# Loading half of x transposed by DMA, fewer remainders of P by DMA, and an output added in place, in a two-problem cached attention kernel

## The chip, the cores and the metric

The kernel runs on one core of one Trainium2 chip. Its time is the time of one execution on the device in microseconds (us). Three runs of the kernel before took 718.01, 720.44 and 720.60 us, with a median of 720.44. Profiles come from one execution each, which the hardware profiler recorded. Engine names in a profile: PE is the matrix engine TensorE (PEld its weight load), DVE is VectorE, ACT is ScalarE, POOL is GpSimd, SP is SyncE, and a "q" behind a name is the engine's queue, which waits and issues DMAs.

## The reference

Two independent problems A and B of the same shape are computed and their outputs stand side by side. B=16 batches, 80 query rows each, D=576, 32 query heads on 16 key/value heads of 512 cached positions, head size 128, all in bf16:

```python
def _A_ref(x, k_cache, v_cache, wq, wo):
    B, Sq, D = x.shape                      # 16, 80, 576
    Hq, Dh = 32, 128
    rep = Hq // k_cache.shape[1]            # 2
    q = (x @ wq).reshape(B, Sq, Hq, Dh).transpose(0, 2, 1, 3)
    k = jnp.repeat(k_cache, rep, axis=1)
    v = jnp.repeat(v_cache, rep, axis=1)
    scores = jnp.einsum("bhqd,bhkd->bhqk", q, k) * (Dh ** -0.5)
    p = _softmax(scores, axis=-1)
    o = jnp.einsum("bhqk,bhkd->bhqd", p, v)
    return o.transpose(0, 2, 1, 3).reshape(B, Sq, Hq * Dh) @ wo
# out = concatenate([A_ref(...), B_ref(...)], axis=-1)   # (16, 80, 1152)
```

## The kernel before

**Steps.** The work is cut into 128 steps, 64 for each problem. One step is one batch with four key/value heads, so 8 query heads of 80 rows, 640 rows in all. A key/value head has 160 query rows: 128 of them are a tile of their own, and the 32 left over of each of the four heads are packed into a fifth tile, the remainder. For each of the five tiles TensorE computes scores of 128 x 512 (L678, the remainder L665), VectorE takes the negative maximum (L687), ScalarE the exponential with the row sum (L691), VectorE the reciprocal (L697), and GpSimd multiplies P by it (L700).

**P turned around.** P times V needs P transposed. For every step TensorE issues small transposes of 64 x 64 blocks against an identity matrix (L733), 8 for each of the five tiles, 40 in a full step; they land in PSUM, and VectorE or ScalarE copies them to `pT` (the four main tiles in two copies, L751 and L752, the remainder in two, L757 and L758). In steps from `RT0` to `RT1` that are odd (`RTM`), the remainder goes another way: SyncE issues a transposing DMA from `p_sb` to `pT` (L740), the step on TensorE has 32 small transposes, and the remainder's two copies are left out. `RT0` is 71, so 27 steps go that way. The remainder's tile of P has four slots (`NPR`), which are used again four steps later. Then come P times V (L781) and the copy of the result to `oT` (L795).

**Projections.** q is projected for four batches and one pair of heads at a time: four matmuls per head over the first 512 of the 576 columns of x (L542, "Q"), and a tail for the last 64 columns (L555, "QT"), in which the two heads use the two halves of the array. Early on, the tails are operations of their own; later they are part of a step's small transposes. The scaled copy to `qT` (L568, L569) is on ScalarE or VectorE. The weights of the first two groups of heads come in four pieces each (L507) with the two tail pieces `wt` (L511).

**x.** The projection needs x transposed, `xT`, in two halves of eight batches (640 rows, five blocks of 128). For problem A a half is loaded plainly into the memory of `acc` (L380) in two parts, three blocks and two; GpSimd doubles the last 64 columns (L388), TensorE transposes the blocks (L401) and the last columns (L419), and VectorE copies them to `xT` (L406, L423). For problem B the first 512 columns come by one transposing DMA for each half (L436), and the last 64 columns by two plain DMAs into `xst` (L441, L442), five transposes (L456) and three copies (L461 to L463).

**Output.** `oT` times wo is summed over two groups of heads (L827). The first group's result is copied to `acc` (L839), the second group's is added to it by VectorE and written as bf16 to a buffer `osb` of two slots (L856), from which SyncE stores it (L862).

**Order.** There is no planner at run time. Every operation is added to a list with a stream's name, and a long string `ORDER` says, letter by letter, which stream's next operation comes next (a digit is the PSUM bank it gets, a quote sends it to the second of two engines). Each engine runs its own operations in that order. Semaphore waits are worked out from what operations read and write. So each engine, TensorE and SyncE's queue too, works strictly in order, and an operation that waits holds all behind it on that engine. At the start SyncE issues the first part of x, the first piece of wq, the second part of x, the rest of the first two groups' wq, and then the first K (L631, a transposing DMA of 1,024 rows by 512).

## Time and profile before

| | us |
|---|---|
| median of three runs | 720.44 |
| the profiled execution | 720.92 |
| its span, first to last instruction | 719.0 |
| TensorE busy | 712.0 (99%) |
| VectorE busy | 630.0 (88%) |
| ScalarE busy | 637.5 (89%) |
| GpSimd busy | 431.9 (60%) |

The page of the profile gives for each engine the busy time and for each group of instructions the count, the mean duration in ns and the idle time just before them with what ended it. "Busy" of TensorE is modelled, since matmuls overlap. Times in rows count from the start of the span. The small transposes of step 64, the first of problem B, start at 375 us, those of step 71 at 416 (its transposing DMA at 413.43), those of step 97 at 555.

### The profile page before, as it was taken

What the parts mean: (1) busy time and instruction counts of PE and PEld (TensorE: products, weight loads), DVE (VectorE), ACT (ScalarE), POOL (GpSimd) and SP (SyncE); (2) the same over time, 40 slices, a digit from 0 to 9 for tenths busy, and PEclk for the clock granted to TensorE, in tenths of its full rate; (3) what the DMA queues carried; (4) which work ended last, traced back from release to release, by engine and by line L of the source; (5) the groups of instructions that cost most, each with busy time, mean ns of one, the idle gap of its engine ahead of it and who ended that gap; (6) DMA issues with size and microseconds to landing.
All of it is one profiled execution on the core that took longest, in us unless ns stands there. A gap on an engine that the chain in (4) does not pass through costs nothing.

```text
span 719.0 us, 25863 instructions
## 1 busy us (share of the span) xinstructions
PE 712.0 (99%) x10604; PEld 508.8 (71%) x10604; DVE 630.0 (88%) x1419; ACT 637.5 (89%) x1830; POOL 431.9 (60%) x650
## 2 busy tenths in 40 slices
PE   9999999999999999999999999999999999999998
PEld 5576777777777777777777776767677777777777
DVE  3999998899978998899998899878898889998995
ACT  1999998899988998799988999888999898998994
POOL 0467657566655765755774566645676466665783
PEclk9999999999999999999999999999999999999999
DMA  9999999999799998999999999999999999999970
GB/s 238 275 217 240 273 252 250 286 232 244 175 268 241 220 241 194 258 223 240 255 216 248 226 201 206 228 246 239 220 229 204 279 196 261 225 247 221 211 195 18
DMA packets 388853, 164.23 MB, mean 228 GB/s; under 512 B 293248, under 2 KB 385664, under 8 KB 388736
## 3 DMA queue, kind: packets, MB, share of 16 engines
q1 hardware_dynamic: 388736, 162.59, 100.2%
q8 instruction: 84, 1.38, 0.8%
q14 instruction: 33, 0.27, 0.2%
HBM read 87.65 MB, written 2.95 MB: 126 GB/s over the span
## 4 chain that ended last, share of the span: by engine, by line
PE 93%; DMA 2%; DVE 2%; ACT 1%; SPq 0%; issue 0%; ACTq 0%; DVEq 0%
PE ps L827 22%; PE ps L781 20%; PE ps L542 18%; PE ps L678 15%; PE ps L733 10%; PE ps L665 5%; PE ps L555 4%; DVE negmax L687 2%; DMA pT<-p_sb 1%; DMA wq_sb<-in_A_wq_dram 1%; DMA out_dram<-osb 1%; ACT p_sb L691 0%; ACT qT L568 0%; DVE xT L406 0%; DVE qT L569 0%
## 5 line engine op out<-in xcount | busy, mean ns | idle before, releaser
L700 POOL TENSOR_SCALAR p_sb<-p_sb,rinv 128x512 bf16<-128x512 bf16 x640 | 430.1, 692 | 271.4 <-DVE rinv L697 270.8
L691 ACT ACTIVATE p_sb<-ps,negmax 128x512 bf16<-128x512 f32 x640 | 442.7, 713 | 27.3 <-DVE negmax L687 23.5
L687 DVE TENSOR_REDUCE negmax<-ps 128x1 f32<-128x512 f32 x640 | 419.2, 682 | 35.0 <-PE ps L678 30.3
L781 PE MATMUL ps<-pT,v_sb 128*128 128x160 bf16 x2048 | 191.2, 233 | 1.1 <-ACT p_sb L691 0.8
L781 PEld LDWEIGHTS ps<-pT,v_sb 128*128 128x128 bf16 x2048 | 152.8, 98 | 42.6 <-ACT p_sb L691 4.1
L827 PE MATMUL ps<-wo_sb,oT 128*128 128x288 bf16 x1280 | 181.1, 286 | 0.0
L678 PE MATMUL ps<-kT,qT 128*128 128x512 bf16 x512 | 178.0, 380 | 1.2 <-ACT p_sb L691 0.8
L542 PE MATMUL ps<-xT,wq_sb 128*128 128x320 bf16 x1024 | 174.4, 299 | 0.2 <-DMA wq_sb<-in_A_wq_dram 0.2
L827 PEld LDWEIGHTS ps<-wo_sb,oT 128*128 128x128 bf16 x1280 | 122.0, 98 | 42.5 <-ACT p_sb L691 0.8
L691 ACT ACTIVATION_READ_ACCUMULATOR p_sb<-ps,negmax 128x1 f32 x640 | 146.0, 228 | 0.0
L542 PEld LDWEIGHTS ps<-xT,wq_sb 128*128 128x128 bf16 x1024 | 95.4, 98 | 45.0 <-ACT p_sb L691 2.4
L751 ACT COPY pT<-ps 128x512 f32<-128x512 f32 x157 | 92.4, 602 | 13.3 <-PE ps L733 12.8
L733 PEld LDWEIGHTS ps<-ident,p_sb 64*128 64x128 bf16 x4904 | 88.2, 95 | 7.3 <-issue 1.3
L733 PE MATMUL ps<-ident,p_sb 64*128 64x64 bf16 x4904 | 92.4, 190 | 0.3 <-issue 0.2
L752 DVE COPY pT<-ps 128x1024 bf16<-128x1024 bf16 x99 | 67.3, 684 | 11.4 <-PE ps L733 10.0
L568 ACT ACTIVATE qT<-ps 128x320 bf16<-128x320 f32 x133 | 59.0, 458 | 19.3 <-PE ps L555 15.5
L569 DVE TENSOR_SCALAR qT<-ps 128x320 bf16<-128x320 f32 x123 | 58.2, 482 | 10.7 <-PE ps L555 6.1
L795 DVE CAST oT<-ps 128x320 bf16<-128x320 f32 x122 | 58.4, 482 | 7.7 <-PE ps L781 7.4
L678 PEld LDWEIGHTS ps<-kT,qT 128*128 128x128 bf16 x512 | 48.0, 97 | 24.1 <-ACT p_sb L691 4.1
L795 ACT CAST oT<-ps 128x320 bf16<-128x320 f32 x134 | 58.9, 451 | 5.2 <-PE ps L781 4.9
L697 DVE RECIPROCAL rinv<-rowsum 128x3 f32<-128x3 f32 (+1 forms) x256 | 38.4, 160 | 1.8 <-ACT p_sb L691 1.7
L665 PE MATMUL ps<-kT,qT 128*32 128x512 bf16 x512 | 39.2, 384 | 0.0
(31 smaller groups left out, 175.5 us busy)
## 6 DMA issues: line engine op xcount, KB each, us to landing
v_sb<-in_A_v_cache_dram SPq DMA_DIRECT2D x64, 512.0 KB, 5.0
v_sb<-in_B_v_cache_dram SPq DMA_DIRECT2D x64, 512.0 KB, 5.2
wo_sb<-in_A_wo_dram SPq DMA_DIRECT2D x8, 576.0 KB, 5.8
wo_sb<-in_B_wo_dram SPq DMA_DIRECT2D x8, 576.0 KB, 5.8
wq_sb<-in_B_wq_dram SPq DMA_DIRECT2D x4, 1024.0 KB, 6.9
out_dram<-osb SPq DMA_DIRECT2D x40, 72.0 KB, 3.8
wq_sb<-in_A_wq_dram SPq DMA_DIRECT2D x8, 256.0 KB, 4.7
wq_sb<-in_A_wq_dram SPq DMA_DIRECT2D x2, 1024.0 KB, 8.4
```

Source lines behind the costliest of these rows:

```text
L542: last = e.matmul(ps[:, vbq[h].phys, QO:QO + 320], lhsT=wq_sb[:, wsl, ck, hi * 128:(hi + 1) * 128], rhs=xT[:, half, ck, n0:n0 + 320], star ...
L665: last = e.matmul(ps[32 * g4:32 * g4 + 32, vb_.phys, :], lhsT=qT[:, qsl_, bl_, g4 * 160 + 128:g4 * 160 + 160], rhs=k_of(U_, g4), start=Tru ...
L678: return e.matmul(ps[:, vb.phys, :], lhsT=qT[:, qsl, bl, gl * 160:gl * 160 + 128], rhs=k_of(U, gl), start=True, stop=True)
L687: return e.tensor_reduce(negmax[:, si:si + 1], ps[:, vb.phys, :], axis=AX.X, op=AluOpType.max, negate=True)
L691: return e.activation(p_sb[:, psl, :], ps[:, vb.phys, :], AF.Exp, bias=negmax[:, si:si + 1], scale=1.0, accum_out=rowsum[:, ss, k:k + 1])
L700: return e.tensor_scalar(p_sb[:, psl, :], p_sb[:, psl, :], rinv[:, ss, k:k + 1], 1.0, op0=AluOpType.mult, op1=AluOpType.mult)
L733: last = e.matmul(dst, lhsT=p_sb[64 * h:64 * h + 64, psls[k_], j * 128:(j + 1) * 128], rhs=ident[64 * h:64 * h + 64, 64 * h:64 * h + 64], ...
L751: return e.copy(dst.bitcast(F32), ps[:, vtp[h].phys, :].rearrange("p (j n) -> p j n", j=4))
L752: return e.tensor_copy(dst, psb[:, vtp[h].phys, :].rearrange("p (j n) -> p j n", j=4))
L781: last = e.matmul(ps[:, vo.phys, off:off + 160], lhsT=v_sb[:, vs, gl, j * 128:(j + 1) * 128], rhs=pT[:, pts, j, :, 32 * gl:32 * gl + 32], ...
L795: return (e.copy if en == "act" else e.tensor_copy)(dst, src)
L827: last = e.matmul(ps[:, vb.phys, 0:DC], lhsT=oT[:, sp_ * (HH // 2) + i, rb * 128:(rb + 1) * 128], rhs=wo_sb[:, 2 * c3 + sp_, i, :], start= ...
```

## The change

Three things change in the code, and the order string is written anew from its first to its last letter.

1. The first half of A's x (eight batches) is no longer loaded plainly and turned on TensorE. The first 512 columns come by two transposing DMAs, for the first three blocks and for the last two, and these are issued on ScalarE's queue. The last 64 columns come as in problem B. The first K, also a transposing DMA but on SyncE's queue, now waits until both have landed. The second half of A's x is loaded as before.
2. `RT0` goes from 71 to 97: the remainders of the odd steps from 71 to 95 go through TensorE; 14 steps are left that use the DMA.
3. The last addition writes its bf16 result into the first half of the memory of the sums that it reads, and the stores read from there; `osb` is gone, and with it the wait for one of its slots.

```diff
-RT0 = 71
+RT0 = 97
+XENG0 = ("act", "act")
...
-        for half in range(NPP):
+        for half in range(1, NPP):
             x_ap = probs[0][0]
...
-        for half in range(NPP):
-            x_ap = probs[1][0]
-
-            def em_ldxt(e, x_ap=x_ap, half=half):
-                src = x_ap.rearrange("b s d -> (b s) d")[half * NROW:(half + 1) * NROW, :]
-                return e.dma_start_transpose(xT[:, half, 0:4, :], src[:, 0:512].rearrange("n (c d) -> n c d", c=4))
+        for xi, (xp, half) in enumerate(((0, 0), (1, 0), (1, 1))):
+            x_ap = probs[xp][0]
+            nm = str(half) if xp else "00"
+            k_ = XA if xi == 0 else 5.0 * (UPR + 16 * half - LQ) - XK[half]
+
+            def em_ldxt(e, k0, k1, x_ap=x_ap, half=half):
+                src = x_ap.rearrange("b s d -> (b s) d")[half * NROW + k0 * 128:half * NROW + k1 * 128, :]
+                return e.dma_start_transpose(xT[:, half, 0:4, k0 * 128:k1 * 128],
+                                             src[:, 0:512].rearrange("n (c d) -> n c d", c=4))
...
+            for part, (k0, k1) in enumerate(((0, 3), (3, 5)) if xi == 0 else ((0, 5),)):
+                S.add(XENG0[part] if xi == 0 else "sp", (-100.0, -85.0)[part] if xi == 0 else k_,
+                      lambda e, k0=k0, k1=k1, f=em_ldxt: f(e, k0, k1),
+                      writes=[R(("xT", half, b_), xp) for b_ in range(k0, k1)], dsem="d_x%d%d" % (half, part),
+                      name="ldxt%s" % nm + (".%d" % part if xi == 0 else ""), stream="xa" if xi == 0 else "x")
...
                 S.add("sp", 5.0 * gfirst[U] + 0.5 * (U - gfirst[U]) - LA - KK, em_ldk,
+                      reads=[R(("xT", 0, b_), 0) for b_ in range(NRT)] if U == 0 else [],
                       writes=[R(("kT", (U + i_) % NK), U + i_) for i_ in range(kw)],
...
-                                return e.tensor_tensor(osb[:, slot, :], ps[:, vb.phys, 0:DC],
+                                return e.tensor_tensor(xs[:, rb, 2 * c3 * DC:(2 * c3 + 1) * DC], ps[:, vb.phys, 0:DC],
                                                        acc[:, rb, c3 * DC:(c3 + 1) * DC], AluOpType.add)
...
-                                return e.dma_start(dst, osb[:, slot, :])
+                                return e.dma_start(dst, xs[:, rb, 2 * c3 * DC:(2 * c3 + 1) * DC])
```

In the new order string TensorE's first operations are: the warm-up, the projection of the first pair of heads, the five transposes of the last columns, the first tail, then the projection of the second pair. Before, they were the warm-up, x's transposes, the projections of three pairs of heads, and then the first three tails. SyncE's first operations are now the first piece of wq, its two tail pieces, the two small loads of x's last columns, the remaining wq, and the first K.

## The prediction

> **What bounds the kernel now.** I read the busy shares of the engines first, then the chain that ended last, then a table of stretches, and only then single rows.

> ```profile
> PE 712.0 (99%) x10604; PEld 508.8 (71%) x10604; DVE 630.0 (88%) x1419; ACT 637.5 (89%) x1830; POOL 431.9 (60%) x650
> PE 93%; DMA 2%; DVE 2%; ACT 1%; SPq 0%; issue 0%; ACTq 0%; DVEq 0%
> core 0: us, PE busy (x) PEld busy (x) DVE busy (x) ACT busy (x) POOL busy (x), PEclk, DMA share, GB/s
> 0.00:7.00 7.00, 5.68 (x32) 3.20 (x33) 1.67 (x6) 1.28 (x1) 1.32 (x8) 1.00 0.75 204
> 7.00:20.00 13.00, 12.48 (x96) 7.42 (x93) 5.15 (x14) 2.52 (x7) 0.00 (x0) 1.00 1.18 264
> 20.00:36.00 16.00, 15.59 (x168) 8.84 (x166) 16.00 (x37) 15.89 (x47) 8.38 (x13) 1.00 1.17 273
> 36.00:413.00 377.00, 376.88 (x5819) 270.98 (x5816) 341.99 (x779) 349.48 (x1012) 233.40 (x349) 1.00 1.03 238
> 413.00:556.00 143.00, 141.33 (x2106) 100.42 (x2104) 125.16 (x277) 130.06 (x374) 91.21 (x136) 1.00 1.04 221
> 556.00:717.00 161.00, 160.05 (x2400) 117.96 (x2397) 140.02 (x311) 138.29 (x392) 97.60 (x146) 1.00 0.94 209
> ```

> TensorE is the bound. Its granted clock is 1.00 throughout, and from 36 to 413 us it is idle 377.00 - 376.88 = 0.12 us. Over 0 to 717 it idles about 5 us in all (the six rows add up to 712.01 busy). So the change can move the end in three places only: the work on TensorE itself, the first 36 us, and the stretch 413 to 556, where it idles 143.00 - 141.33 = 1.67 us. That stretch holds steps 71 to 97, whose odd steps send their remainders by DMA today.

> **The remainders, steps 71 to 97.** Thirteen odd steps (71, 73 ... 95) go back to TensorE: 8 more small transposes each, and two evictions in place of one DMA.

> ```profile
> 690.16 0.69 PE ps L733 x40
> 694.00 0.57 PE ps L733 x32
> L757 ACT COPY pT<-ps 128x128 f32<-128x128 f32 x106 | 28.5, 284 | 7.6 <-PE ps L733 7.0
> L758 DVE COPY pT<-ps 128x256 bf16<-128x256 bf16 x96 | 26.1, 283 | 7.3 <-PE ps L733 6.5
> ```

> In the chain a step with 40 transposes takes 0.69 us and one with 32 takes 0.57. TensorE gets 13 x 0.12 = 1.56 us more, all on the path. The 26 evictions are 26 x 0.284 = 7.4 us over VectorE and ScalarE. In 413 to 556 these two have 286 - 125.16 - 130.06 = 30.8 us free, which is the cover, and I cost them at nothing: from 36 to 413 every remainder goes through TensorE and it still never waits. If the cover were gone, half of them on either engine would be 3.7 us.

> What leaves with the 13 DMAs is their waits: two pieces of the chain, an issue, and the three TensorE rows after them.

> ```profile
> 413.43 4.13 DMA pT<-p_sb
> 510.62 5.67 DMA pT<-p_sb
> 478.87 1.23 SPq L740 DMA_TRANSPOSE pT<-p_sb  x1
> 418.48 0.39 PE L678 MATMUL ps<-kT,qT 128*128 128x512 bf16 x1 [0.17 <-ACT p_sb L691]
> 483.85 0.44 PE L781 MATMUL ps<-pT,v_sb 128*128 128x160 bf16 x4 [0.81 <-ACT p_sb L691]
> 517.21 0.39 PE L678 MATMUL ps<-kT,qT 128*128 128x512 bf16 x1 [0.46 <-ACT p_sb L691]
> ```

> The first and third follow a transfer that held a slot of P which the next exponential wanted. Before the second stands the DMA issued at 478.87: 483.85 is 5 us later, like the 4.13 and 5.67 above, and the row names ScalarE, which had long been done. I take out 0.17 + 0.81 + 0.46 = 1.44 us; the rest of the 1.67 has other causes. What is late next is TensorE's own work. So this part is +1.56 - 1.44 = +0.12 us, and SyncE's queue loses 13 issues that nobody waits for.

> **The start.** SyncE loses two x loads and gains two small loads of the last 64 columns; ScalarE, idle then, gains the two transposing loads. TensorE loses 25 transposes and gains 5; GpSimd loses two copies; VectorE loses 7 copies and gains 3. Nothing was behind GpSimd's. In SyncE's queue, the next fence, 0.45 and 0.50 go and about as much comes in, so what stands behind keeps its time but for the wait below.

> ```profile
> 0.79 0.45 SPq L380 DMA_DIRECT2D acc<-in_A_x_dram  x1
> 1.30 0.48 SPq L507 DMA_DIRECT2D wq_sb<-in_A_wq_dram  x1
> 1.82 0.50 SPq L380 DMA_DIRECT2D acc<-in_A_x_dram  x1
> 2.37 1.38 SPq L511 DMA_DIRECT2D wt<-in_A_wq_dram  x2
> ...
> 10.01 5.71 SPq L631 DMA_TRANSPOSE kT<-in_A_k_cache_dram  x1
> 3.79 4.45 DMA wq_sb<-in_A_wq_dram
> 8.37 2.33 PE L542 MATMUL ps<-xT,wq_sb 128*128 128x320 bf16 x16 [0.16 <-DMA wq_sb<-in_A_wq_dram]
> 19.45 0.38 PE L678 MATMUL ps<-kT,qT 128*128 128x512 bf16 x1 [0.36 <-ACT qT L568]
> 19.76 0.31 PE L555 MATMUL ps<-xT,wt 64*128 64x320 bf16 x2
> ```

> Now the second piece of the projection goes on at 8.37, when its weights have landed (3.79 + 4.45), and the first scores start at 19.45. In the new order the first projection tail comes before the second piece's matmuls. TensorE works in order, so everything behind that tail waits for the small loads, five transposes and three copies. Their prices are those of the same operations for problem B:

> ```profile
> xst<-in_B_x_dram SPq DMA_DIRECT2D x1, 80.0 KB, 4.1
> xT<-in_B_x_dram SPq DMA_TRANSPOSE x1, 7.1
> xst<-in_B_x_dram SPq DMA_DIRECT2D x1, 16.0 KB, 7.6
> 237.83 0.44 PE L456 MATMUL ps<-ident,xst 128*128 128x128 bf16 x5
> 238.95 0.47 DVE L461 COPY xT<-ps 64x640 bf16<-64x640 bf16 x1
> ...
> 239.79 0.22 DVE L463 COPY xT<-ps 64x128 bf16<-64x128 bf16 x1
> kT<-in_A_k_cache_dram SPq DMA_TRANSPOSE x1, 9.3
> DMA to landing us min/median/max: 6.1/8.4/13.4
> acc<-in_A_x_dram SPq DMA_DIRECT2D x2, 288.0 KB, 4.6
> ```

> The small loads are issued after wq's first piece and two of wt: 0.79 + 0.48 + 1.38 and gaps, about 2.8, the second at 3.4 (I give each of them 0.6, near wt's 1.38 / 2). Landing takes between 4.1 and 7.6 us by the two xst rows. I take 4.1, since the 7.6 stood behind megabytes of another load and here only 384 KB are ahead: 7.5. Then 0.44 for the transposes, 239.79 + 0.22 - 238.95 = 1.06 for the copies, 0.3 for the tail: the second piece's matmuls start at 9.3, 0.9 later than 8.37. From there to the first scores it is 11.08 us now; one more tail (0.31) comes ahead of the scores, in place of the 0.36 that TensorE waited there. Scores at 20.3, so +0.85.

> The other bound is the first K. Its load now waits for both transposing loads, and every K, V and x load behind it on SyncE's queue waits with it. SyncE itself reaches it at about 10.2 (14 issues ahead, as now). The transposing loads are issued on ScalarE at 0.79 and, at an issue time between P's 1.23 (128 rows) and K's 5.71 (1,024 rows), about 3.3. With B's 7.1 the second lands at 10.4, K at 10.4 + 9.3 = 19.7: 0.6 us before it would matter. The bounds of that load are 4.6 (the plain x load) and 13.4 (the slowest K).

> From the first scores to 36 us VectorE is busy 16.00 of 16.00. The new order has about one 0.6 us reduction less before the second transposing step there; TensorE's idle time in that row is 0.41, so I take back 0.2. The start is +0.85 - 0.2 = +0.65 us.

> **Output in place.** The adder writes where it reads, and the two-slot buffer goes.

> ```profile
> L856 DVE TENSOR_TENSOR osb<-ps,acc 128x288 bf16<-128x288 f32 x40 | 17.9, 450 | 7.1 <-PE ps L827 6.1 <-PE ps L781 0.5
> ```

> Its waits end on TensorE (6.1 + 0.5 of 7.1), not on a store, so freeing the slots gives at most 0.5 us in idle VectorE time: zero.

> **The sum.** 1.56 - 1.44 + 0.65 = +0.77 us. The profiled execution took 720.92 us (span 719.0), 0.48 above the median of 720.44. So 721.7 for such an execution, 721.2 for the median.

> **The rivals.**
> First, slower: the small loads land late and hold the first tail. For it: TensorE's order leaves no way round, and one of B's took 7.6. Against: the other took 4.1. At 7.6 the scores start 3.5 us later: 724.7. It exceeds +0.5% when the second small load lands after about 10.3.
> [...]

> Second, slower: K is late. If the second transposing load takes K's own 9.3, it lands at 12.6, K at 21.9, scores at 22.0: 722.9. At 13.4 it is 726.9. It passes +0.5% once that load lands after 13.8.
> [...]

> Third: the waits at 413 to 556 do not leave, because the whole order is rewritten and puts others there. Then 1.44 stays: 722.6.

> Fourth, the start costs nothing: the small loads land by 6.6 and the tail hides before 8.37, 0.4 is gained in 20 to 36: 1.56 - 1.44 - 0.4 = -0.3, so 720.1.

> **How the numbers follow.** Forecast 0.50, first rival 0.12, second 0.13, third 0.13, fourth 0.12. A change of 0.5% is 3.6 us, about what runs from 718.01 to 720.6 can tell: 716.8 and 724.0 are the bounds. Slower by more: 0.07 from the first, 0.05 from the second, 0.05 from the rest, 0.17. Faster by more: even all 5 us of TensorE's idle time less the 1.56 gives 717.0, so 0.05 for what the trace does not show. Within: 0.78. The range is 717.8 (the fourth, less the run to run spread) to 725.0 (the first rival's bound).

> **What would show it.** In the profile after: TensorE's busy time in the stretch of steps 71 to 97 up by about 1.5 us and its idle time there near 0.2; 14 DMAs of P for 27; the first scores near 20.3 with the tail's copies just ahead of the second piece's matmuls; stores and their adders unchanged. The prediction is wrong if the first scores start before 19 or after 22, if TensorE idles over 1 us between the 36th us and the steps from 97 on, or if the work per step on TensorE differs outside the thirteen steps.

## The result, and the profile after

The changed kernel took 725.26 us, the median of three runs (723.76 to 725.92), against 720.44 before: a ratio of 1.0071, with a 95% interval from 1.0049 to 1.0093. It is slower by 4.8 us. The prediction was 721.2 us, its range ended at 725.0, and a change within 0.5% had been given 78%.

The profiled execution took 725.92 us, with a span of 722.9 (before: 720.92 and 719.0). So 3.9 of the 5.0 us between these two executions lie in the span, and 1.1 outside it, where the trace shows nothing. First the busy times and the chain that ended last, from the page of the kernel after; then the table of stretches, whose columns are those shown for the kernel before (line numbers are up to 9 higher than there).

```profile
PE 712.7 (99%) x10688; PEld 508.6 (70%) x10688; DVE 628.2 (87%) x1421; ACT 642.6 (89%) x1850; POOL 431.6 (60%) x648
...
PE 95%; DVE 2%; ACT 1%; DMA 1%; issue 0%; SPq 0%
```

```profile
0.00:7.00 7.00, 4.32 (x16) 1.74 (x16) 0.27 (x1) 1.28 (x1) 0.68 (x6) 1.00 0.86 190
7.00:20.00 13.00, 11.59 (x89) 6.86 (x89) 4.62 (x12) 2.70 (x8) 0.00 (x0) 1.00 1.21 278
20.00:36.00 16.00, 15.44 (x167) 8.56 (x166) 15.58 (x36) 15.72 (x48) 8.01 (x14) 1.00 1.19 237
36.00:413.00 377.00, 376.37 (x5809) 270.29 (x5808) 340.46 (x774) 348.53 (x1013) 234.66 (x350) 1.00 1.04 239
413.00:556.00 143.00, 142.65 (x2185) 103.21 (x2183) 127.15 (x287) 135.00 (x393) 89.50 (x134) 1.00 0.91 220
556.00:721.00 165.00, 162.33 (x2432) 117.99 (x2430) 140.10 (x315) 139.36 (x392) 98.76 (x147) 0.99 0.89 195
```

The reader sees three things. From 413 to 556 us the change did what was forecast: TensorE's idle time fell from 1.67 us to 143.00 - 142.65 = 0.35. From 556 on, where nothing was expected, it idles 165.00 - 162.33 = 2.67 us, and the granted clock is 0.99. In the first 20 us it is busy 4.32 + 11.59 = 15.9 us instead of 18.2, because x's transposes are gone and it waits there instead; that looks harmless.

Where the late loss sits is shown by TensorE's timeline of the kernel after near 648 us, by SyncE's queue at the same place, and by a table of stretches there:

```profile
645.45 0.59 PE L687 MATMUL ps<-kT,qT 128*128 128x512 bf16 x2
648.08 0.99 PE L790 MATMUL ps<-pT,v_sb 128*128 128x160 bf16 x12 [2.04 <-issue]
648.91 0.49 PE L687 MATMUL ps<-kT,qT 128*128 128x512 bf16 x1
649.20 2.13 PE L836 MATMUL ps<-wo_sb,oT 128*128 128x288 bf16 x8
```

```profile
640.27 0.98 SPq L643 DMA_DIRECT2D v_sb<-in_B_v_cache_dram  x2
641.29 1.19 SPq L749 DMA_TRANSPOSE pT<-p_sb  x1
```

```profile
647.00:652.00 5.00, 3.92 (x25) 2.71 (x26) 2.21 (x4) 3.11 (x9) 1.14 (x2) 0.70 1.01 194
652.00:657.00 5.00, 5.00 (x77) 3.13 (x76) 3.66 (x10) 2.20 (x5) 3.06 (x5) 0.95 0.47 141
```

Step 113's remainder is one of the fourteen that still go by DMA. Its DMA was issued at 641.29, behind two loads of V, and landed at 647.99, after 6.7 us where the median of the fourteen is 3.5. P times V of this step started 0.09 us later; the page says "issue" because the releaser it looked for had long been done. TensorE idled 2.04 us, and the granted clock fell to 0.70 in the five microseconds that follow: eight matmuls of L836 took 2.13 us, where eight elsewhere take 1.15. That is about 3.8 us in one place, an estimate: 2.04 of idling and, from the clock column, 5 x 0.30 + 5 x 0.05 = 1.75 of lost speed. In the profile of before the same DMA landed with 3.25 us to spare.

### The profile page after: what moved, and what is told of

Its sections match the earlier page's. It is cut to its first block, busy times and chain, and to the rows that moved or that the text cites. A ratio compares the mean times of both kernels' runs of the same rounds, so it can differ in the third digit from the quotient of the medians.

```text
span 722.9 us, 26016 instructions
## 1 busy us (share of the span) xinstructions
PE 712.7 (99%) x10688; PEld 508.6 (70%) x10688; DVE 628.2 (87%) x1421; ACT 642.6 (89%) x1850; POOL 431.6 (60%) x648
## 3 DMA queue, kind: packets, MB, share of 16 engines
q8 instruction: 84, 1.38, 0.8%
## 4 chain that ended last, share of the span: by engine, by line
PE 95%; DVE 2%; ACT 1%; DMA 1%; issue 0%; SPq 0%
PE ps L836 22%; PE ps L790 20%; PE ps L550 19%; PE ps L687 16%; PE ps L742 10%; PE ps L674 5%; PE ps L563 4%; DVE negmax L696 1%; DMA xst<-in_A_x_dram 1%; ACT p_sb L700 0%; DVE xT L407 0%; SPq L519 0%; DVE pT L761 0%; ACT pT L760 0%; PE ps L463 0%
## 5 line engine op out<-in xcount | busy, mean ns | idle before, releaser
L790 PE MATMUL ps<-pT,v_sb 128*128 128x160 bf16 x2048 | 189.1, 233 | 2.0 <-issue 2.0
L836 PE MATMUL ps<-wo_sb,oT 128*128 128x288 bf16 x1280 | 182.4, 287 | 0.0
L836 PEld LDWEIGHTS ps<-wo_sb,oT 128*128 128x128 bf16 x1280 | 121.7, 98 | 42.8 <-issue 1.5
L742 PEld LDWEIGHTS ps<-ident,p_sb 64*128 64x128 bf16 x5008 | 89.8, 95 | 7.7 <-issue 1.4
L742 PE MATMUL ps<-ident,p_sb 64*128 64x64 bf16 x5008 | 93.9, 190 | 0.6 <-issue 0.6
L576 ACT ACTIVATE qT<-ps 128x320 bf16<-128x320 f32 x146 | 65.0, 462 | 15.1 <-PE ps L563 12.0
L804 DVE CAST oT<-ps 128x320 bf16<-128x320 f32 x127 | 60.7, 481 | 6.7 <-PE ps L790 6.2
L804 ACT CAST oT<-ps 128x320 bf16<-128x320 f32 x129 | 57.0, 453 | 6.1 <-PE ps L790 5.7
L577 DVE TENSOR_SCALAR qT<-ps 128x320 bf16<-128x320 f32 x110 | 52.3, 481 | 11.0 <-PE ps L563 6.6
L563 PE MATMUL ps<-xT,wt 64*128 64x320 bf16 x256 | 39.0, 307 | 1.2 <-DVE xT L470 1.2
```

The costliest lines, as they stand in the source:

```text
L563: last = e.matmul(ps[:, vbq[h].phys, QO:QO + 320], lhsT=wt[64 * h:64 * h + 64, wsl, hp, :], rhs=xT[64 * h:64 * h + 64, half, 4, n0:n0 + 32 ...
L742: last = e.matmul(dst, lhsT=p_sb[64 * h:64 * h + 64, psls[k_], j * 128:(j + 1) * 128], rhs=ident[64 * h:64 * h + 64, 64 * h:64 * h + 64], ...
L790: last = e.matmul(ps[:, vo.phys, off:off + 160], lhsT=v_sb[:, vs, gl, j * 128:(j + 1) * 128], rhs=pT[:, pts, j, :, 32 * gl:32 * gl + 32], ...
L804: return (e.copy if en == "act" else e.tensor_copy)(dst, src)
L836: last = e.matmul(ps[:, vb.phys, 0:DC], lhsT=oT[:, sp_ * (HH // 2) + i, rb * 128:(rb + 1) * 128], rhs=wo_sb[:, 2 * c3 + sp_, i, :], start= ...
```

## The experiments

All comparisons are of medians; a timeline, and the time of the first scores in the tables, is that of one execution. The kernels of one batch ran on the same chip with their own runs of the kernel before, whose medians were 720.37 (e1 to e4), 721.0 (e5 to e8), 720.41 (e9 to e12) and 720.87 (e13 to e15). "Order" means the string that says which operation comes next.

### First batch: is it step 113?

**e1**, the kernel after once more.

> The changed kernel as it is, to see whether what its profile shows comes back. Theory T (the transposing DMA of step 113 stands behind two V loads in SyncE's queue, TensorE waits for it and then loses clock): step 113's P times V waits again, 1 to 2.5 us, and the time is 723.5 to 726. Theory R (the loss is a little everywhere in the rewritten order): the time is the same, but the wait at step 113 may be absent, and the stretches from 36 us on are each a little longer.

**e2**, after with step 113's remainder through TensorE:

```diff
-rtr = RT0 <= U < RT1 and (RTM[U % 2] or U >= RT2)
+rtr = RT0 <= U < RT1 and (RTM[U % 2] or U >= RT2) and U != 113
```

> The changed kernel with the remainder of step 113 alone sent back through TensorE (8 small transposes and two evictions more, one DMA less; nothing else moves). T: the wait of 2 us is gone and with it the stretch of lower clock, +0.12 us of TensorE work, so 1.5 to 3.5 us faster than the changed kernel, 721.5 to 723.5. R: the same as the changed kernel within 0.5 us.

**e3**, the order of after to step 95 and then the order of before, whose remainders from 97 on also go by DMA:

```diff
-NPR = 4
+NPR = 5
 ORDER: after's as far as step 95, then before's
```

> The changed kernel's order up to step 95, from there the order of the kernel before (one slot more for P's remainders, which the cut needs). T: the end part costs what it cost before, and what is left is the start (+0.45 us) and steps 71 to 95 (about -1): 719.5 to 721. R: the first part carries its share of the loss: 722 to 724.

**e4**, the reverse: before's x and order to step 95, with `RT0` at 97, then after's order.

> The other way round: the order of the kernel before up to step 95, with its remainders of steps 71 to 95 through TensorE and the output in place, from there the changed kernel's order. T: the wait at step 113 is there, 723 to 726. R: half of the loss, 721 to 723.

| | median | ratio to before, 95% interval |
|---|---|---|
| e1 after again | 727.32 | 1.0097, 1.0078 to 1.0117 |
| e2 113 by TensorE | 724.58 | 1.0058, 1.0040 to 1.0076 |
| e3 after, then before | 724.23 | 1.0053, 1.0038 to 1.0069 |
| e4 before, then after | 731.73 | 1.0157, 1.0140 to 1.0174 |

Step 113's DMA is worth 2.7 us (e1 to e2), but without it the kernel is still 4.2 us slower than before, so my theory T of that batch holds for a part only. Two things limit the 2.7. In the profile of e1, the fastest of its six executions, step 113 does not wait at all, which is the sign that theory R had named. And about 0.9 us of it lie outside the span: e1's executions have 2.5 to 2.9 us there, e2's 1.7 to 1.8, for a reason that no run here shows; by the median spans (724.6 and 722.85) the DMA is worth 1.75. e3 has none of the late order and is still 3.9 us slower, so a large part lies ahead of step 97; but 1.16 us of it, in its profile, is a stop at 548 us, near the place where its two orders meet, and neither parent has one there.

e4 tells little about T: TensorE waits 0.42 us for step 113's DMA there, but most of the loss is elsewhere. I had put 26 evictions by hand into an order written without them, and TensorE waits on VectorE and ScalarE in many places, as the waits of e4 from 425 to 560 us show (columns: total us, times, longest):

```profile
PE ps L677 <- ACT qT L567: 1.5, 2, 0.9
PE ps L541 <- ACT acc L838: 1.0, 1, 1.0
PE ps L677 <- ACT pT L750: 0.8, 2, 0.5
PE ps L780 <- DVE rinv L696: 0.6, 1, 0.6
```

It does say that the cover which the prediction counted on (30.8 us free on these two engines) is of use only in an order that is written for it. After's own order is: 0.35 us of idling there.

In e1's profile the loss was at the start, in a form that the table of stretches hides. TensorE's timeline of e1:

```profile
1.24 3.60 PE L354 MATMUL ps<-wo_sb 128*128 128x512 bf16 x8 [1.24 <-DVE wo_sb L347]
6.01 2.29 PE L550 MATMUL ps<-xT,wq_sb 128*128 128x320 bf16 x8 [1.18 <-DMA xT<-in_A_x_dram]
8.10 0.74 PE L463 MATMUL ps<-ident,xst 128*128 128x128 bf16 x5
9.99 0.45 PE L563 MATMUL ps<-xT,wt 64*128 64x320 bf16 x2 [1.16 <-DVE xT L470]
10.38 3.38 PE L550 MATMUL ps<-xT,wq_sb 128*128 128x320 bf16 x12
```

and the same place in the kernel after:

```profile
1.24 3.21 PE L354 MATMUL ps<-wo_sb 128*128 128x512 bf16 x8 [1.24 <-DVE wo_sb L347]
5.89 1.25 PE L550 MATMUL ps<-xT,wq_sb 128*128 128x320 bf16 x8 [1.44 <-DMA xT<-in_A_x_dram]
7.39 0.45 PE L463 MATMUL ps<-ident,xst 128*128 128x128 bf16 x5 [0.25 <-DMA xst<-in_A_x_dram]
9.00 0.31 PE L563 MATMUL ps<-xT,wt 64*128 64x320 bf16 x2 [1.16 <-DVE xT L470]
9.24 1.80 PE L550 MATMUL ps<-xT,wq_sb 128*128 128x320 bf16 x12
...
19.99 0.60 PE L687 MATMUL ps<-kT,qT 128*128 128x512 bf16 x2
```

The waits are the same, 1.2 to 1.4 us for x and 1.16 for the copies. But in e1 the first eight matmuls take 2.29 us instead of 1.25, and the twelve behind the first tail 3.38 instead of 1.80: half speed until 13.8 us. The first scores start at 22.75 us in e1 and at 19.99 in the profile of after. Six profiles of kernels with this start (after, e1, e2, e3, e5, e9) have 19.99, 22.75, 20.93, 20.48, 22.57 and 22.73; before had 19.45.

The PEclk column says 1.00 at this place in five of the six. The trace keeps the clock as a list of changes, and the column counts all that is ahead of the first change as 1.00. That first change, to full speed, stands at 3.93 us in after, 5.46 in e3, 9.19 in e2, 13.31 in e5 and 13.83 in e1, just where the durations change too; in the kernel before it stands at 6.44. In e9 the clock was full from 3.99 us, fell back at 7.40, behind a stop of 1.99 us, and was full again at 14.23. There the column shows it; TensorE's timeline of e9, and a row of its table of stretches:

```profile
6.47 1.42 PE L550 MATMUL ps<-xT,wq_sb 128*128 128x320 bf16 x8 [1.99 <-DMA xT<-in_A_x_dram]
8.02 0.71 PE L463 MATMUL ps<-ident,xst 128*128 128x128 bf16 x5
10.27 3.38 PE L550 MATMUL ps<-xT,wq_sb 128*128 128x320 bf16 x12
```

```profile
8.00:12.00 4.00, 2.82 (x14) 1.59 (x15) 1.95 (x6) 0.00 (x0) 0.00 (x0) 0.50 1.22 278
```

Why it differs between executions no run shows: full speed comes between 3.93 and 13.83 us behind the same eight warm-up matmuls, which took 3.21 us in after, 3.24 in e9 and 3.60 in e1. Whether a longer warm-up brings it sooner is asked in the second batch.

### Second batch: the start alone, the rest alone, and a longer warm-up

**e5** has after's load of x and its order to step 21, then before's order with `RT0` at 71. **e6** is the reverse: before's x and order to step 17, then after's order with `RT0` at 97 and the output in place.

> The new load of x and its order up to step 21, then the order of before, remainders by DMA from step 71 on again; the whole computation is done. Theory C (the loss sits largely at the start: TensorE has nothing between the warm-up and the first projection, waits again before the first tail, and in most executions runs the first projections at half speed): the profile of after had 1.2 us more lost at the start than before, the repetition of after 3.75 us, so 721.6 to 724.2, and in a slow execution the first eight projection matmuls take 2.3 us instead of 1.25. Theory O (the start costs the 0.65 us of the prediction, and the loss is made behind step 21 by the rewritten order and the DMA of step 113): 720.6 to 721.2.

> The other half: x as in before with its order to step 17, then the order of after, remainders by DMA from step 97 on, output in place; the whole computation is done. Theory C: no loss at the start, what is left are the stops near 333 us and 531 us (0.8 and 0.7 us) and the late DMA of step 113 (0 to 2 us) against the waits gone in the middle (1.4 us) and 1.6 us of added transposes: 720.5 to 723. Theory O: nearly all the loss of after, 724 to 727.

**e7** and **e8** are the kernel after with

```diff
-NWARM = 8
+NWARM = 12
 ORDER (e8 only): the first tail QT0 behind the fourth Q operation, not behind the second
```

> After with 12 warm-up matmuls instead of 8, so that TensorE is busy from 1.2 us until about 5.8 us, when the first piece of x lands; the whole computation is done. Theory C: the first eight projection matmuls take 1.25 us in every execution, and the time falls by 1 to 2.5 us against the 725.3 and 727.3 of after: 723.5 to 725.5. Theory O: no change, 725.3 to 727.3.

> The same with 12 warm-up matmuls, and the first tail of the Q projection behind the second pair of projections instead of ahead of it, so that TensorE has work while the small loads are transposed and copied; the whole computation is done. Theory C: the 1.2 us of idling before the first tail goes as well: 722.3 to 724.3, and the first scores start near 19 us instead of 20. Theory O: no change, 725.3 to 727.3.

| | median | ratio to before, 95% interval | first scores, us |
|---|---|---|---|
| e5 start alone | 721.47 | 1.0012, 0.9993 to 1.0032 | 22.57 |
| e6 rest alone | 721.90 | 1.0016, 1.0003 to 1.0030 | 18.64 |
| e7 12 warm-ups | 727.17 | 1.0088, 1.0065 to 1.0111 | 20.68 |
| e8 and the tail later | 725.32 | 1.0058, 1.0037 to 1.0080 | 21.15 |

Neither half gives the whole, and they do not add up: 0.5 and 0.9 us for the halves, 4.8 to 7.0 for both. (e5's median lies just below what theory C had expected and just above what theory O had; its first eight matmuls take 2.29 us, as C said.) e5 shows how. In its profile the first scores are 3.1 us late, but step 112's transposes only 1.0, and the end 0.8. What comes back is the stretch with the waits that the prediction had read from the kernel before; the stretch in e5:

```profile
413.00:556.00 143.00, 143.00 (x2112) 102.26 (x2105) 127.69 (x284) 132.85 (x380) 91.12 (x135) 1.00 1.02 226
```

TensorE does not idle there at all, where it idled 1.67 us before, though `RT0` is 71 as before. Step 83's DMA of P, on which it had waited 0.81 us, is issued 2.78 us later than before (481.65 against 478.87) but lands only 1.06 us later (484.82 against 483.76), and 0.83 us before it is wanted. So the start's loss and the waits in the middle are not two terms to be added: in before's order a late start is in part paid out of those waits, and the change removes these waits as well, so that nothing is left to pay it from. Why this DMA landed faster when issued later (3.17 us against 4.89), whether the loads ahead of it had had more time, was not tested by itself.

e7 and e8 miss theory C's expectation; their medians lie where theory O had them. The clock at the start was mended only in part (in e7 three of the first eight matmuls are still slow), and the late losses were the worst of all. Beside 2.65 us at step 113 in e7 and 1.59 in e8, TensorE stops in both near 617 us before a projection, and for 1.5 and 1.2 us at 88 us, by what the last section describes. In e8 ScalarE's timeline, and the issue in SyncE's queue that I put it down to:

```profile
614.33 0.69 ACT L700 ACTIVATE p_sb<-ps,negmax 128x512 bf16<-128x512 f32 x1
...
616.86 0.69 ACT L700 ACTIVATE p_sb<-ps,negmax 128x512 bf16<-128x512 f32 x1 [1.74 <-DVE negmax L696]
```

```profile
611.24 2.02 SPq L749 DMA_TRANSPOSE pT<-p_sb  x1
```

That DMA, step 107's, landed at 616.77, after 5.5 us, and the exponential that writes the next remainder into its slot starts 0.09 us later, while the same exponential in the profile of after ran without any wait. ScalarE's queue stands behind it, and TensorE loses 1.40 us (1.02 in e7, 0.59 in e2, 0.42 in e1, none in after).

### Third batch: without the DMAs of the steps 107 and 113

```diff
+ and U not in (107, 113)
```

**e9** is after with this, **e10** also has e8's warm-up and tail, **e11** is e6 with it (start of before), and **e12** is the kernel before with the output in place and nothing else.

> After with the remainders of the steps 107 and 113 alone by TensorE; the other DMAs of P stay where they are. Theory P (beside the start, what is lost late is lost to these two DMAs of P, which land behind loads of K and V: TensorE waits 0.4 to 1.4 us near 617 us for an exponential that needs step 107's buffer, and up to 2.7 us near 648 us for step 113, once with the clock at half behind it): 1.5 to 4 us less than after, 722.5 to 724.5. Rival (the delay moves to the next DMA of P or to other places): 725 or more, with a new stop at steps 105, 109, 111 or 115.

> The same with 12 warm-up matmuls and the first tail behind the second pair of projections. Theory P: start and late part mended, 721 to 723; near the time of before, since what is left are the stops of TensorE at blocks of its instructions (0 to 2 us) and 1.7 us of added transposes against the waits of before that are gone. Rival: 725 as the run with the later tail.

> The start of before to step 17, then the order of after with the remainders of 107 and 113 by TensorE, the other late ones by DMA, output in place. Theory P: 1 to 1.5 us less than the run with the rest alone (721.9), 720.2 to 721; a version as fast as before, not faster than it by more than 0.3%. Rival: 721.9 or more.

> Before with the sums of the output written in place of the buffer of their own, and nothing else changed. Both theories: no change, 720 to 721.5, the sums stay beside TensorE's work and the stores read what the sums wrote.

| | median | ratio to before, 95% interval | first scores, us |
|---|---|---|---|
| e9 after without 107, 113 | 724.59 | 1.0053, 1.0036 to 1.0070 | 22.73 |
| e10 and the start of e8 | 724.44 | 1.0053, 1.0036 to 1.0070 | 21.34 |
| e11 start of before | 720.92 | 1.0004, 0.9993 to 1.0016 | 18.88 |
| e12 in place alone | 720.90 | 1.0006, 0.9991 to 1.0022 | 19.40 |

This batch separates the parts. e11 has everything of the change but the start and two DMAs, and is as fast as before. e9 differs from e11 in the start alone and is 724.59 - 720.92 = 3.7 us slower; in their profiles the first scores are 22.73 - 18.88 = 3.85 us apart, and the ends of TensorE's work 3.62: here the loss goes through to the end undiminished. The two DMAs cost 721.90 - 720.92 = 1.0 us behind before's start (in e6's profile TensorE waits 1.17 us for step 113's) and 727.32 - 724.59 = 2.7 behind the new one. These four medians come from three batches, whose runs of before differ by up to 0.6: each against its own runs of before, it is 0.4 and 2.8, the 0.4 within the uncertainty, and 1.8 of the 2.8 by the spans. Nor did the stop near 617 us go with step 107's DMA: in e9, e10, e11 and e13 TensorE still stops there for 0.6 us, now until the copies of that step's remainder are done, which I had put on one engine. The output in place costs nothing that can be measured. e10 misses: putting the tail later only moved the waiting (1.0 us before the next projection).

### Fourth batch: is it the clock or the waiting?

**e13** is e9 with TensorE kept busy. Twelve warm-up matmuls instead of eight, and five more of them between the transposes of the small loads and the first tail:

```diff
-NWARM = 8
+NWARM = 12
+NFILL = 5
...
+        def em_fill(e, vw=vw):
+            last = None
+            for _ in range(NFILL):
+                last = e.matmul(ps[:, vw.phys, :], lhsT=ones, rhs=warm, start=True, stop=True)
+            return last
```

**e14** is the kernel before with `NWARM = 1`. **e15** is e11 with `NPR = 5` and the two evictions of step 107's remainder on two engines.

> The kernel without the DMAs of the steps 107 and 113 (new load of x, 724.6 us), with 12 warm-up matmuls and five more of them between the transposes of the small loads and the first tail, so that TensorE idles nowhere long at the start. Theory C (the clock): the first projections and those behind the first tail run at full speed, the first scores start at 20 to 20.5 us instead of 22.7, and the time falls to 722 to 723. Rival (it is the wait for x and for the copies, not the clock): first scores at 20.7 to 21.3 us as in the runs with 12 warm-up matmuls, and 724 to 725.

> Before with one warm-up matmul instead of eight, nothing else changed: the clock alone, without the new load. Theory C: TensorE's first transposes and projections run at half speed until some 3 to 4 us of work lie behind it, the first scores start at 20.5 to 22 us instead of 19.45; the end is later by 0 to 2 us, 720.4 to 722.5, since the run with the new load in before's order lost 3.1 us by the first scores and 0.9 us at the end. Rival (the half speed has to do with the new load, not with idling): first scores at 19.4 us, 720.4.

> The start of before, the order of after, no DMA of P for 107 and 113 (720.9 us), with five buffers for P's remainders instead of four and the two evictions of step 107 on two engines instead of one. Expected: the stop of 0.8 us near 614 us goes, 720 to 720.6; a version that beats before by more than 0.5% is not expected from any theory.

| | median | ratio to before, 95% interval | first scores, us |
|---|---|---|---|
| e13 filled | 722.77 | 1.0026, 1.0010 to 1.0042 | 20.40 |
| e14 one warm-up | 721.64 | 1.0015, 0.9999 to 1.0030 | 19.32 |
| e15 best | 719.16 | 0.9983, 0.9966 to 1.0000 | 18.29 |

TensorE's timeline of e13; L367 is the filling:

```profile
1.24 4.51 PE L355 MATMUL ps<-wo_sb 128*128 128x512 bf16 x12 [1.24 <-DVE wo_sb L348]
6.12 1.25 PE L558 MATMUL ps<-xT,wq_sb 128*128 128x320 bf16 x8 [0.37 <-DMA xT<-in_A_x_dram]
7.79 0.45 PE L471 MATMUL ps<-ident,xst 128*128 128x128 bf16 x5 [0.42 <-DMA xst<-in_A_x_dram]
8.08 1.24 PE L367 MATMUL ps<-wo_sb 128*128 128x512 bf16 x5
9.41 0.31 PE L571 MATMUL ps<-xT,wt 64*128 64x320 bf16 x2
9.65 1.80 PE L558 MATMUL ps<-xT,wq_sb 128*128 128x320 bf16 x12
```

Work that computes nothing makes this kernel faster. Eight matmuls take 1.25 us and twelve 1.80, the first scores come 2.3 us earlier than in e9, and against their own runs of before the loss falls from 4.2 to 1.9 us (by the ratios from 0.53% to 0.26%, 1.9 us). One profile shows one execution, and e9's fell back to half speed while e13's is among the fastest of its twelve, but the medians over 6 and 12 runs agree with it; the two intervals still overlap a little, so the size is known to a us or two only. So of the start's 3.7 us about 2 are TensorE's speed. The remaining 1.4 (1.9 us slower than before, against 0.5 for e11) go with the 1.5 us by which e13's first scores are later than e11's; I read that as the waiting for x and the copies, which filling does not shorten.

In e14, with the old load of x, the half speed shows too:

```profile
4.49 1.44 PE L401 MATMUL ps<-ident,acc 128*128 128x128 bf16 x12 [2.65 <-DMA acc<-in_A_x_dram]
5.73 0.52 PE L419 MATMUL ps<-ident,acc 128*128 128x128 bf16 x3
6.58 1.01 PE L401 MATMUL ps<-ident,acc 128*128 128x128 bf16 x8 [0.32 <-DMA acc<-in_A_x_dram]
```

The eight transposes at 6.58 take 1.01 us, and 0.61 in the kernel before. So the half speed does not need the new load. That the stop of 2.65 us prolonged it is not shown by this pair: the first twelve transposes of the kernel before run at half speed as well, and in e11, with eight warm-up matmuls and no such stop, so do all but the last two of the eight (two rows of before, one of e11):

```profile
4.63 1.49 PE L401 MATMUL ps<-ident,acc 128*128 128x128 bf16 x12
6.51 0.61 PE L401 MATMUL ps<-ident,acc 128*128 128x128 bf16 x8
```

```profile
6.23 0.95 PE L400 MATMUL ps<-ident,acc 128*128 128x128 bf16 x8
```

The size was missed too: full speed came by about 8 us (6.44 in before, 6.93 in e11), the first scores start at 19.32 us, not later than before's 19.45, where I had expected 20.5 to 22, and the 0.8 us at the end is within the uncertainty. TensorE has small waits of its own there (0.16 and 0.36 us in the rows of before); I read the missing loss as paid out of those. By 8 us TensorE had worked about 3.8 us in e14 (0.61 of the warm-up, 4.49 to 6.25, and 6.58 to 8), inside the expected 3 to 4; but by the first change of the clock it had worked 3.93 - 1.24 = 2.7 us in after, 6.44 - 1.24 = 5.2 in before, and about 10.3 in e1 (3.60, 6.01 to 8.84, and 9.99 to 13.83). These are estimates from the rows, and no fixed amount of work shows in them.

e15 is faster than after by 6 us. Its median is below that of before and below the range that I had expected, and the stop near 614 us is gone; but its gain on before is 0.17%, and the interval touches 1. It does not contain the new load of x.

## Why the prediction was wrong, point by point

**The start, +0.65 us: the step that failed.** By 3.7 against 0.65 us it is the largest miss. The landings that counted were right: the small loads landed at 7.04 and 7.34 (said: 7.5), the first tail started at 9.00, the second piece at 9.24 (9.3), the first K landed at 17.5 and held nobody (19.7, with the second transposing load at 7.6 for 10.4; those loads took 5.0 and 5.4 us, nearer to the plain load's 4.6 than to the 7.1 that I had used). In the profile of after the first scores start at 19.99 (20.3). That agreement is the luck of one execution, whose clock was full from 3.93 us; in e1, e5 and e9 they start at 22.75, 22.57 and 22.73, past the 22 that the prediction had named as a sign of being wrong. What failed is the unspoken assumption in "from there to the first scores it is 11.08 us now", that the matmuls behind a wait take what they took before. I had read "granted clock is 1.00 throughout" from the table and not asked what keeps it there: x's 25 transposes, which I counted as work that leaves, were what kept TensorE going from 4.6 us to the first projection. They ran at half speed themselves until 6.44 (twelve in 1.49 us, and behind it eight in 0.61), and the projections, from 6.96, at full speed (eight in 1.25); behind the new load it is mostly the projections that do, and in e1 TensorE needs about 3.1 us more for the same work than in after (1.04 + 0.29 + 0.14 + 1.58, from the four pairs of rows). That TensorE's own work keeps its clock up is my reading. e13 speaks for it, with 1.25 and 1.80 us for the eight and the twelve matmuls where work was put in, against 1.42 and 3.38 in e9.

**The 0.2 us taken back between 20 and 36 us: failed, and small.** TensorE's idle time in that row rose from 0.41 to 0.56 us. A stop for an exponential gave way to a longer one, for VectorE's copy of the second half of x, which TensorE still transposes (a row of before and of after); all ten kernels with the new start have it, with 0.52 to 0.54 us.

```profile
33.24 0.39 PE L678 MATMUL ps<-kT,qT 128*128 128x512 bf16 x1 [0.22 <-ACT p_sb L691]
```

```profile
32.55 0.39 PE L687 MATMUL ps<-kT,qT 128*128 128x512 bf16 x1 [0.54 <-DVE xT L407]
```

**The remainders, +0.12 us.** The idle time in 413 to 556 fell by 1.32 us (said: 1.44, and near 0.2 left; 0.35 was left). The part as a whole, in e11 with its two DMAs taken out, is within the uncertainty of nothing. That the evictions are covered was right for after's own order. That the 1.44 us is a gain of its own was wrong: with the new start alone (e5) those waits are gone anyway.

**"What is late next is TensorE's own work": failed.** Next were the DMAs of P that stayed, at the steps 107 and 113. The diff's last 14 DMAs looked untouched, but the order around them was new, and so was what SyncE issues just ahead of them. The prediction gave no price to anything behind step 97; it was 0.4 to 2.8 us in the medians, and about 3.8 in one execution.

**Output in place, zero.** Right (e12).

**The rivals.** The first two, late small loads and a late K, are out by the landings; the small loads, in pieces of 128 B, landed in 4.0 and 4.3 us here, near the 4.1 that the forecast used. The third comes nearest: other waits came for the ones removed, but at 334 and 648 us (near 617 in the repetition) and at the start, not in the stretch it named. The fourth is out. No rival had TensorE's speed in it, and the chance of a loss over 0.5% was put at 17%.

## What to carry to other kernels

Work that leaves an engine may have been what kept that engine at speed: when preparatory work on TensorE is replaced by a DMA, allow for matmuls behind the new gap at nearly twice their time (in e1 they took 2.29 us for 1.25, and 3.38 for 1.80, until 13.83 us, 7.8 us behind the first of them), and at the start read durations, not the clock column. A loss early and a wait later are not two terms of a sum: the loss may be paid out of the wait, or the wait may have hidden it. When an order is rewritten, look at each transfer that stays for what is newly issued ahead of it.

## What the runs showed of the hardware that was not expected

Short stops of TensorE with "issue" as their cause turned up in nearly all kernels. One in before and one in after, from the timelines (a row each of before and of after):

```profile
474.72 0.30 PE L733 MATMUL ps<-ident,p_sb 64*128 64x64 bf16 x9 [0.24 <-issue]
```

```profile
334.14 0.29 PE L742 MATMUL ps<-ident,p_sb 64*128 64x64 bf16 x8 [0.62 <-issue]
```

The page of before has a queue of the kind "instruction" whose packets go with TensorE's list in number:

```profile
q8 instruction: 84, 1.38, 0.8%
```

The other is the clock. At the start the PEclk column can say 1.00 while matmuls run at half speed (in e1 from 8.10 to 13.70 us, where twelve took 3.38 us), since the list of changes behind it begins with the first change; at 647 us it shows 0.70 for the same thing. The changes in after lie 645.12, 3.41 and 71.68 us apart, which is 189, 1 and 21 times 3.413 us; those in e9 above lie 3.41 and 6.83 us apart, 1 and 2 times. Once full, the clock fell behind three stops of TensorE, of 1.99 (e9), 2.04 (after) and 2.65 us (e7), and behind none of up to 1.59 us (e8). What decides between 1.6 and 2.0 us, the length or where the stop lies, was not tested.
